# Moving six state factors to TensorE and four transposes to DMAs in a recurrent attention and MoE kernel

## The chip, the cores and the metric

The kernel runs on one core of a Trainium2 chip. The metric is the device time of one execution in microseconds (us), as the median of several runs. The engines are called as the profile calls them: PE (matrix multiplications), PEld (its weight loads), DVE (element by element), ACT (functions and copies), POOL (element by element, and it issues some DMAs) and SP, which here only issues DMAs.

## The reference

```python
# q, k, v, alpha: 4 batches, 8 heads, 768 steps, 48 wide
for t in range(S):
    state = alpha[:, :, t, :, None] * state + np.einsum('bhd,bhe->bhde', k[:, :, t], v[:, :, t])
    y[:, :, t] = np.einsum('bhd,bhde->bhe', q[:, :, t], state)
x = np.ascontiguousarray(attn_out.transpose(0, 2, 1, 3)).reshape(B * S, H * D)   # 3072 x 384
h = x @ w_in                  # 384 x 2048
r = np.maximum(h, 0.0)
out = ((r * r) @ w_out)       # 2048 x 384, float32
```

## The kernel before

**Chunks.** The recurrence is done in 24 chunks of 128 steps, six for each batch. In a chunk the decays are summed as logarithms: ACT takes the logarithm of alpha (line 438), PE multiplies it with a triangle of ones (448), and ACT takes the exponentials of the sums and of their negatives (467 and 471). DVE multiplies them into q and k (495 or 498, 501). q and k are then turned, so that the head dimension lies on the partitions: as eight PE transposes (276) and a DVE copy out of PSUM (395), or by one transposing DMA that SP issues (515). PE makes the scores, DVE masks them (570), PE multiplies them with v and adds q times the state before (both at 273, through a helper). The state is updated by a matmul, multiplied by the decay over the whole chunk (DVE, 604) and copied as bf16 (ACT, 609). ACT copies the chunk's result out of PSUM as x (393 or 414's operand `xn`), and x is turned too: by three PE transposes and a copy, or by a transposing DMA (414).

The decay over a whole chunk, the state factor `ae`, comes in one of two ways. For chunks below `TURN` four matmuls with a single column of ones (450) sum the logarithms, and two small exponentials on ACT (474, 477) write the factors. From `TURN` on the exponential is written as float32 in another order (`Af`, 467), and two small DMAs issued by POOL (484) take its last row. Chunks from `XFROM` on turn q and k by DMA, chunks from `XTURN` on turn x by DMA.

**The first four chunks** are done as two super-chunks of 256 steps (`add_super`), in which every partition holds two steps; their loads are `add_load2` (388), and the copies of the turned q and k are `e_cp` (line 717, costs in line 724), on the engine that the schedule finds free first.

**MoE.** The tokens' first layer is done for groups of chunks (`GN`: four, one, one, then two at a time). A relu on ACT (878) and a square on DVE (886) follow each PSUM bank; then the second layer with the weights in `w_out_b`. ACT copies the result into one of four `held` tiles of four chunks each (953), which share a ring of four buffers with the loads of the weights, and POOL issues the output DMAs (961, 964), the last few SP.

**Order.** A list scheduler in the kernel (`Plan`) sets the order of the instructions on each engine before anything is emitted. Each operation has an engine, or several with a cost for each, an estimated duration, what it depends on and a priority. `gate` keeps the chunks from running further ahead of the MoE than a lead that grows from 3.5 to 6.5 chunks. `OUT_AT + 2.0 * s` is the time in the schedule before which the output of chunk `s` isn't placed; on the chip it only sets its place in POOL's order. `DMA_ORDER` is the order of the first loads on SP. Each engine, and SP as the queue of DMAs, then works through its list in order and waits on semaphores where data isn't there. Before the second layer begins, matmuls on a constant (`warm`) fill holes that the schedule sees on PE.

Of the kernel before, what the change touches and what calls it, by code (L numbers as in the profile page):

```python
# [59 lines left out]
def after(op, x=0.0):  # L60
    return (op, x)
# [103 lines left out]
def kernel(  # L165
# [86 lines left out]
    w_out_b = consts.tile([P, FT, d_model], BF16)  # L252

    NBUF = 4
    TURN = 12
    AE_LAT = 3.6
    L_s = big.tile([P, NBUF, H, DP], BF16)
    nc.gpsimd.memset(L_s[:, :, :, D:], 0.0)
# [10 lines left out]
    def pin(ins):  # L269
        tc.keep_in_program_order(ins)  # L270

    def mm(*a, **kw):
        pin(nc.tensor.matmul(*a, **kw))  # L273
# [23 lines left out]
    def add(eng, dur, emit, *deps, **kw):  # L297
        return plan.add(Op(eng, dur, emit, deps, **kw))
# [47 lines left out]
    SRC = dict(srcs)  # L346
    EARLY = 2 * 3
    PAIRS = 8
    XFROM, XTURN = 12, 14
    LEAD = 3.5  # L350

    NS = 2
# [38 lines left out]
    def cast(op, out_t, in_t):  # L391
        if op.eng == "ACT":
            pin(nc.scalar.copy(out_t, in_t))  # L393
        elif op.eng == "DVE":
            pin(nc.vector.tensor_copy(out_t, in_t))  # L395
        else:
            pin(nc.gpsimd.tensor_copy(out_t, in_t))
# [29 lines left out]
    def add_chunk(s):  # L427
# [18 lines left out]
        def e_p0():  # L446
            pm = d["pm"] = psum(p0, [P, 512], FP32)
            mm(pm[:, 0:HD], lhsT=utri_b[:, 0, :], rhs=L[:, :, 0:D], start=True, stop=True)
            for p in range(NP if s < TURN else 0):
                mm(pm[:, HD + p:HD + p + 1], lhsT=L[:, 2 * p:2 * p + 2, :], rhs=ones_col,  # L450
                   start=True, stop=True)
        p0 = Op("PE", 0.27 if s < TURN else 0.17, e_p0, [ln], takes=GLA_BANKS, lat=0.17, **g)
        p0.gla = s
        d["p0"] = p0

        def split(x, s):
            if s < TURN:
                return x.rearrange("p (h d) -> p h d", h=H)
            return x.rearrange("p (n j d) -> p n j d", n=NP, j=2)

        def e_A():
            if s < TURN:
                d["A"] = work.tile([P, H, D], BF16, name="A")
            else:
                d["Af"] = work.tile([P, 2, D, NP], FP32, name="Af", bufs=2)
                d["A"] = d["Af"].rearrange("p j d n -> p n j d")
            pin(nc.scalar.activation(d["A"], split(d["pm"][:, 0:HD], s), AF.Exp))  # L467
# [10 lines left out]
        plan.add(p0)  # L478
        a_ = add("ACT", 0.38 if s < TURN else 0.76, e_A, p0, **g)
        ai = add("ACT", 0.38, e_Ai, p0, after(a_), **g)  # L480

        def e_aed():
            for j in range(2):
                pin(nc.gpsimd.dma_start(out=ae_s[HF * j:HF * j + D, i, j], in_=d["Af"][P - 1:P, j]))  # L484
        if s < TURN:
            ae0 = add("ACT", 0.18, e_ae0, p0, after(ai), **g)
# [147 lines left out]
    def add_super(u):  # L634

        d = SUP[u]
        i = 2 * u % NBUF
# [3 lines left out]
        g = dict(prio=-10.0 + u * 0.02)  # L641
# [67 lines left out]
        def e_p1(v, w, src):  # L709
            if w == 0:  # L710
                d["pT"][v] = psum(p1[v], [P, 2, NH, 2, 2, HF], BF16)
            for t in any_:
                for n in range(NH):
                    p = NH * v + n
                    tr(d["pT"][v][:, w, n, :, t, :], src[:, t, 2 * p:2 * p + 2, :], ident_bf)

        def e_cp(v):
            d["qk"][v] = work.tile([P, 2, NH, 2, 2, HF], BF16, name="qkT")
            cast(cp[v], d["qk"][v], d["pT"][v])
        p1, cp = [None, None], [None, None]  # L720
        for v in any_:
            p1[v] = plan.add(Op("PE", 0.225, lambda v=v: e_p1(v, 0, qA), [mq[v]], takes=SUP_BANKS, lat=0.15, **g))
            p1k = plan.add(Op("PE", 0.225, lambda v=v: e_p1(v, 1, kI), [mk[v], after(p1[v])], lat=0.15, **g))
            cp[v] = add({"DVE": 0.61, "ACT": 0.92}, 0, lambda v=v: e_cp(v), p1k, **g)
            p1[v].gives = cp[v]
        cq = cp[1]

# [114 lines left out]
    NGT = 3  # L842
    FIRST = sl_bank[4:1:-1]
    M2_LAST = sl_bank[::-1]
    OUT_AT = 118.0
    LAST_COLS = ((0, 256), (256, 384))
    RELU_PRIO = -20.0
    RELU_PRIO0 = 0.0
# [74 lines left out]
    def add_moe2(g, tt, before, box, quarters, pools):  # L923
# [41 lines left out]
        if s < NT - 3:  # L965
            add("POOL", 0.56, e_out, ev, at=OUT_AT + 2.0 * s, lat=2.5, prio=5.0).dma = 0.77
        else:
            add("OUT", 0.55, e_out, ev)
        return op

    DMA_ORDER = ["0 at0 qt0 kt0 at1 qt1 kt1 vt", "1 at0 at1 qt0 kt0 qt1 kt1", "i", "1 vt"] + ["i"] * 5 + ["o"] * 4
    for x in DMA_ORDER + [s for s in range(2 * NS, NT) if s not in DMA_ORDER]:
        if x in ("i", "o"):
            load_w(x)
        elif isinstance(x, str):
            for nm in x[1:].split():
                add_load2(int(x[0]), nm)
            if len(SUP[int(x[0])]) == 2 * len(srcs) - 1:
                add_super(int(x[0]))
        else:  # L980
            for nm, _ in srcs:
                add_load(x, nm)
            add_chunk(x)
# [84 lines left out]
```

## Time and profile before

| | us |
|---|---|
| median of 3 runs (lowest to highest) | 179.23 (179.03 to 179.42) |
| the profiled execution | 179.80 |
| its span, first to last instruction | 178.1 |
| PE busy / weight loads busy | 172.0 / 126.3 |
| DVE / ACT / POOL busy | 124.8 / 122.8 / 53.1 |

The granted clock was 0.999 over the span. Of PE's time, the first layer's matmuls took 72.0 us and the second's 69.8 as the rows count them. The rows of matmuls overlap, since each lasts until its result is out; where the text speaks of what a matmul costs, it takes the distance from its start to the next start. The DMA loads of q, k, v and alpha are 192 KB for each chunk and tensor.

### The profile page before, as it was taken

How to read it: one execution, taken by the hardware profiler on the slowest of the kernel's cores; microseconds unless marked ns; L12 is line 12 of the kernel's file. 1: busy time of each engine (PE TensorE's matmuls, PEld its weight loads, DVE VectorE, ACT ScalarE, POOL GpSimd, SP SyncE). 2: the span in 40 equal slices, each digit the busy share in tenths (PEclk: the TensorE clock that was granted, in tenths of full speed). 3: DMA queues.
4: the chain of work that ended last, by engine and by line, in shares of the span. 5: the costliest groups of instructions: out<-in, count | busy, mean ns of one | idle time of the engine just before them, and what ended most of it. 6: DMA issues, size and time to landing. Idle time of an engine off the chain costs nothing.

```text
span 178.1 us, 4801 instructions
## 1 busy us (share of the span) xinstructions
PE 172.0 (97%) x1866; PEld 126.3 (71%) x1867; DVE 124.8 (70%) x256; ACT 122.8 (69%) x263; POOL 53.1 (30%) x95
## 2 busy tenths in 40 slices
PE   7999999999999999999999999899999999999993
PEld 3567684566896788878766786686688867757862
DVE  6699769936799798998986976798248933800600
ACT  4557789456898689979956698874598947522821
POOL 6023467711110211115222233327736080212000
PEclk9999999999999999999999999999999999999999
DMA  5999999999998999988999799999999969232012
GB/s 128 275 271 322 311 352 377 247 194 213 216 185 156 213 184 203 229 176 155 125 214 209 144 209 109 187 193 239 212 204 294 211 162 212 69 91 89 0 44 88
DMA packets 115798, 34.34 MB, mean 193 GB/s; under 512 B 109840, under 2 KB 114064, under 8 KB 115776
## 3 DMA queue, kind: packets, MB, share of 16 engines
q1 hardware_dynamic: 113536, 29.89, 81.5%
q0 software_dynamic: 2240, 4.15, 7.3%
q8 instruction: 14, 0.23, 0.6%
q14 instruction: 8, 0.07, 0.1%
HBM read 25.17 MB, written 4.72 MB: 168 GB/s over the span
## 4 chain that ended last, share of the span: by engine, by line
PE 79%; DMA 7%; DVE 4%; SPq 3%; ACT 3%; issue 1%; ACTq 0%; DVEq 0%
PE bank L273 71%; PE bank L276 4%; SPq L388 3%; DMA qt<-in_q_dram 3%; DMA at<-in_alpha_dram 3%; PE sc L273 2%; PE st L273 2%; DMA kt<-in_k_dram 2%; ACT r L878 1%; DVE sm L570 1%; ACT Af L467 1%; DVE qkT L395 1%; ACT xn L393 0%; DVE sm L763 0%; DVE xT_big L395 0%
## 5 line engine op out<-in xcount | busy, mean ns | idle before, releaser
L273 PE MATMUL bank<-xT_big,w_in_b 128*128 128x256 bf16 (+2 forms) x599 | 72.0, 268 | 0.3 <-ACT r L878 0.2
L273 PE MATMUL bank<-w_out_b,gT 128*128 128x384 bf16 (+2 forms) x400 | 69.8, 319 | 0.0
L878 ACT ACTIVATE r<-bank 128x512 bf16<-128x512 f32 x96 | 57.0, 611 | 13.5 <-PE bank L273 11.5
L886 DVE TENSOR_TENSOR gT<-r 128x512 bf16<-128x512 bf16 x96 | 46.1, 514 | 23.7 <-ACT r L878 23.4
L273 PEld LDWEIGHTS <-w_in_b 128*128 128x128 bf16 x600 | 53.2, 98 | 11.2 <-issue 1.1
L273 PEld LDWEIGHTS <-gT 128*128 128x128 bf16 x400 | 37.1, 98 | 19.4
L443 POOL CAST vb<-vt 128x384 bf16<-128x384 f32 x20 | 11.1, 553 | 58.1 <-DMA vt<-in_v_dram 30.8
L953 ACT COPY held<-bank 128x384 f32<-128x384 f32 x22 | 10.6, 481 | 14.9 <-PE bank L273 14.6
L484 POOL DMA_DIRECT2D ae_s<-Af x24 | 12.2, 511 | 25.4 <-ACT Af L467 22.2
L570 DVE TENSOR_TENSOR sm<-sc,utri_b 128x512 bf16<-128x512 f32 x24 | 15.4, 684 | 2.0 <-PE sc L273 1.8
L273 PEld LDWEIGHTS <-qkT 64*128 64x128 bf16 (+2 forms) x304 | 10.5, 97 | 5.1 <-issue 2.4
L393 ACT CAST xn<-bank 128x384 bf16<-128x384 f32 x24 | 11.1, 485 | 4.4 <-PE bank L273 4.1
L498 DVE TENSOR_TENSOR qk_s<-qt,Af 128x384 bf16<-128x384 f32 x12 | 10.2, 854 | 4.6 <-ACT Af L467 4.6
L438 ACT ACTIVATE L_s<-at 128x384 bf16<-128x384 f32 x20 | 10.6, 543 | 2.7 <-DMA at<-in_alpha_dram 2.7
L961 POOL DMA_DIRECT2D out_dram<-held x17 | 9.2, 545 | 7.9 <-ACT held L953 7.9
L467 ACT ACTIVATE Af<-bank 128x384 f32<-128x384 f32 x12 | 10.6, 883 | 0.9 <-PE bank L273 0.7
L501 DVE TENSOR_TENSOR qk_s<-kt,Ainv 128x384 bf16<-128x384 f32 x20 | 11.0, 548 | 0.0
L395 DVE COPY qkT<-bank 128x1024 bf16<-128x1024 bf16 (+1 forms) x14 | 8.3, 609 | 3.4 <-PE bank L276 3.4
L609 ACT CAST sb<-st 128x384 bf16<-128x384 f32 x16 | 8.0, 499 | 3.9 <-DVE st L604 3.8
L471 ACT ACTIVATE Ainv<-bank 128x384 bf16<-128x384 f32 x20 | 10.3, 514 | 0.0
L570 DVE TENSOR_TENSOR sm<-bank,utri_b 128x512 bf16<-128x512 f32 x16 | 10.2, 681 | 0.0
L604 DVE TENSOR_TENSOR st<-st,ae_s 128x384 f32<-128x384 f32 x16 | 8.9, 557 | 1.7 <-PE st L273 1.7
(71 smaller groups left out, 165.6 us busy)
## 6 DMA issues: line engine op xcount, KB each, us to landing
at<-in_alpha_dram SPq DMA_DIRECT2D x24, 192.0 KB, 4.0
qt<-in_q_dram SPq DMA_DIRECT2D x24, 192.0 KB, 3.8
kt<-in_k_dram SPq DMA_DIRECT2D x24, 192.0 KB, 4.0
vt<-in_v_dram SPq DMA_DIRECT2D x20, 192.0 KB, 3.9
out_dram<-held POOLq DMA_DIRECT2D x17, 192.0 KB, 4.5
wo<-in_moe_w_out_dram SPq DMA_DIRECT2D x4, 768.0 KB, 7.3
wi<-in_moe_w_in_dram SPq DMA_DIRECT2D x4, 384.0 KB, 6.8
wi<-in_moe_w_in_dram SPq DMA_DIRECT2D x2, 768.0 KB, 5.6
```

What stands on the lines that cost most here:

```text
L273: pin(nc.tensor.matmul(*a, **kw))
L393: pin(nc.scalar.copy(out_t, in_t))
L438: pin(nc.scalar.activation(L[:, :, 0:D], d["at"], AF.Ln))
L443: pin(nc.gpsimd.tensor_copy(d["vb"], d["vt"]))
L467: pin(nc.scalar.activation(d["A"], split(d["pm"][:, 0:HD], s), AF.Exp))
L471: pin(nc.scalar.activation(d["Ai"], d["pm"][:, 0:HD].rearrange("p (h d) -> p h d", h=H), AF.Exp, scale=-1.0))
L484: pin(nc.gpsimd.dma_start(out=ae_s[HF * j:HF * j + D, i, j], in_=d["Af"][P - 1:P, j]))
L501: pin(nc.vector.tensor_mul(kI[:, :, 0:D], d["kt"], d["Ai"]))
L570: pin(nc.vector.tensor_mul(d["sm"][:, hh], d["sc"][hh], utri_b.to_broadcast([P, NP, P])))
L878: pin(nc.scalar.activation(box["r"][:, 0:w], box["ph"][:, 0:w], AF.Relu))
L886: pin(nc.vector.tensor_mul(gT[g][:, f0:f0 + per, lo * P:lo * P + n], r, r))
L953: pin(nc.scalar.copy(box["ob"], box["po"]))
```

## The change

The two ways of making the state factor, and of turning q, k and x, keep their code; the chunks from which they apply are set anew. Chunks 12 to 17 take their state factors from one-column matmuls and two exponentials, with the exponential of the sums in bf16. Chunks 10 and 11 turn q and k by DMA, chunks 12 and 13 turn x by DMA. The copies of the second half of the turned q and k of both super-chunks go to ACT alone. The outputs stand 16 us later in the schedule. The load of super-chunk 1's v stands ahead of the first part of `w_in`, not behind it. The scheduler works all orders out anew.

```diff
-    TURN = 12
+    TURN = 18
...
-    XFROM, XTURN = 12, 14
+    XFROM, XTURN = 10, 12
...
-            cp[v] = add({"DVE": 0.61, "ACT": 0.92}, 0, lambda v=v: e_cp(v), p1k, **g)
+            cp[v] = add({"ACT": 0.92} if (u, v) in [(0, 1), (1, 1)] else {"DVE": 0.61, "ACT": 0.92}, 0, lambda v=v: e_cp(v), p1k, **g)
...
-    OUT_AT = 118.0
+    OUT_AT = 134
...
-    DMA_ORDER = ["0 at0 qt0 kt0 at1 qt1 kt1 vt", "1 at0 at1 qt0 kt0 qt1 kt1", "i", "1 vt"] + ["i"] * 5 + ["o"] * 4
+    DMA_ORDER = ["0 at0 qt0 kt0 at1 qt1 kt1 vt", "1 at0 at1 qt0 kt0 qt1 kt1 vt", "i"] + ["i"] * 5 + ["o"] * 4
```

## The prediction

> **What bounds the kernel now.** I read the busy digits first, then the DMA lines of the page, the chain of waits, and last the timeline where PE's starts stand apart.
>
> ```profile
> PE   7999999999999999999999999899999999999993
> ...
> DMA  5999999999998999988999799999999969232012
> ...
> q1 hardware_dynamic: 113536, 29.89, 81.5%
> ...
> PE 79%; DMA 7%; DVE 4%; SPq 3%; ACT 3%; issue 1%; ACTq 0%; DVEq 0%
> ```
>
> PE is full from the second slice to the end, and the DMA engines are full nearly as long, to about 150 us. So there are two limits. PE's own work sets the end as long as something is ready for it; the DMA engines set when the chunks get ready. A busy digit can hide a wait, so I took the distances between the starts of PE's matmuls against the usual distance of each shape. From 27 us on the matmuls stand at that distance (109 ns for 256 columns, 162 ns for 384), except at 45.3 (0.29 us lost), 69.9 (0.25), 112.7 to 113.2 (0.78) and some of 0.1 to 0.2. About 1.8 us in all: not much is left to win there, and every new wait is paid in full. In the timeline the largest one reads so:
>
> ```profile
> 101.43 1.65 SPq L515 DMA_TRANSPOSE qkT<-qk_s  x1
> ...
> 104.42 2.96 SPq L414 DMA_TRANSPOSE xT_big<-xn  x2
> ...
> 107.44 0.57 SPq L368 DMA_DIRECT2D at<-in_alpha_dram  x1
> ...
> 112.13 0.52 ACT L438 ACTIVATE L_s<-at 128x384 bf16<-128x384 f32 x1 [1.07 <-DMA at<-in_alpha_dram]
> 112.56 1.06 ACT L878 ACTIVATE r<-bank 128x512 bf16<-128x512 f32 x2
> ```
>
> Chunk 20's alpha is issued on SP behind three transposing DMAs, lands 4.7 us later, and ACT stands 1.07 us at its logarithm with the relus queued behind. PE waits first for the logarithm (0.46), then for a relu (0.32).
>
> The start has the other stretch where PE is not fed:
>
> ```profile
> 17.37 0.96 POOL L656 CAST vb<-vt 128x384 bf16<-128x384 f32 x2 [1.16 <-DMA vt<-in_v_dram]
> ...
> 18.36 0.51 PE L273 MATMUL st<-vb,qk_s 64*128 64x96 bf16 x8
> ...
> 19.11 0.81 PE L273 MATMUL bank<-warm 128*128 128x512 bf16 x3 [0.24 <-ACT r L878]
> ```
>
> The second v lands at 17.4 us, its cast frees the state matmuls at 18.36, and PE does matmuls on a constant meanwhile.
>
> **Part by part. PE work.** One chunk in the timeline gives the prices by start to start:
>
> ```profile
> 58.07 0.39 PE L276 MATMUL bank<-ident_bf,qk_s 128*128 128x128 bf16 x4
> ...
> 58.29 0.33 PE L273 MATMUL bank<-L_s,utri_b 128*128 128x384 bf16 x1
> ...
> 58.45 0.24 PE L273 MATMUL bank<-ones_col,L_s 128*128 128x1 bf16 x4
> ...
> 58.56 0.38 PE L276 MATMUL bank<-ident_bf,qk_s 128*128 128x128 bf16 x4
> ```
>
> Four transposes hold PE for 0.22 us (58.07 to 58.29), four one-column matmuls for 0.11 (58.45 to 58.56; 0.10 in other chunks). Removed: two groups of four in chunks 10 and 11 (4 x 0.22 = 0.88) and three x transposes at 0.165 in chunks 12 and 13 (0.33). Added: 6 x 0.105 = 0.63. Net -0.58 us, on the engine that sets the end.
>
> [...] The trace has load rows of 96 to 100 ns but starts 25 ns apart, since the loads run under the matmuls before.
>
> **ACT and DVE.** In six chunks the 883 ns exponential (L467) becomes the 495 ns one and two of 0.17 us are added: -0.05 us each on ACT. The q product falls from 854 to 565 ns: -1.7 us on DVE, which also loses two copies of 685 ns and two of 351 ns. DVE is 70% and ACT 69% busy and neither ends the chain, so I count nothing; the cover is PE's MoE work, without it q and k of each chunk would come 0.7 us earlier. Twelve small DMAs leave POOL (6.1 us of its time), which is 30% busy; nothing.
>
> **The two copies forced to ACT** (L724). The first ran on DVE at 9.98 us, the second at 16.36. ACT has no row of this size; by its rows of 265, 372, 481 ns for 128, 256, 384 elements 1024 take about 1.0 us, against 0.69. Scores come 0.15 to 0.35 us later, the mask products on DVE 0 to 0.6 us earlier, and the logarithms of super-chunk 1 (10.35, 11.10) may queue up to 0.5 behind. Bounds -0.6 to +0.5; taken as 0, the copies being nearest to an even trade.
>
> **Second v before w_in.** v moves past one 384 KB load. That load landed at 15.3 and v 2.05 us later, so v comes 1.2 to 2 us earlier and the first w_in some 2 us later. Its cast then ends near 18.2 instead of 16.2, and the first MoE matmuls go from 17.6 to about 18.3, up to 0.65 us. The fifth w_in load waits for that cast's buffer, but three loads ahead of it land until 20.7, which hides it; without them its landing (22.7) would slip 2 us. Chunk 3's x, which PE awaits at 24.27 (0.29 us), can come up to 1.9 us earlier. What is late next is chunk 4: its logarithm waits for DMA until 34.48 whatever the start does, and its x arrives at 45.12, just as the first group's MoE work runs out (45.2). Chunk 4's first matmul comes 1.6 us after its logarithm ends (36.62 against 35.0), so at most 1.6 us can be kept. Bounds -1.6 to +0.65; I take -0.4, nearer to the 0.29 that PE visibly waits than to the end.
>
> **Four more transposing DMAs.** SP spends at least 1.25 us issuing one of q and k and 1.19 one of x, 4.9 in all. From the DMA packets (256 B, mean 28 ns, 1024 per q and k, 384 per x, 16 engines) they take 1.8 and 0.68 us of all engines: 5.0 us where the DMA share by stage is 0.98 to 1.11 (60 to 100 us). They land 4.4 and 4.0 us after issue (medians), against 1.3 for q and k on PE and DVE (eight transposes 0.61, copy 0.69) and 0.7 for x. Queued behind them on SP are the loads of chunks 14 to 20. Chunks 16, 17 and 18 have slack between logarithm and first matmul (8.9, 10.5 and 5 us); 15, 19 and 20 have 1.2, 1.2 and 0.6. Bounds: -0.8, if the new order removes the stall at 112.7, to +5.0, if nothing hides them. I take 0, nearest to that stall staying as it is, and keep the ends.
>
> **Outputs 16 us later in POOL's order.** Between 120 and 140 us their packets take 6.8 us of the DMA engines; most of that moves later, and the last loads gain it. Their buffers are a ring of four: eviction 16 (144.9) waits for outputs 0 to 3. By the order of POOL now, outputs 0 and 1 would issue before the v cast at 136.2 and 2 and 3 right behind, landed by 142: 3 us of cover; without it ACT and the relus wait. Some twelve outputs run together after 152.6, beside the last x transposes (155.5, 156.8), but 48 matmuls (155.2 to 163.0) hide those.
>
> **Sum.** -0.58 - 0.4 = -0.98 us. On the profiled execution, 179.80 (span 178.1 and 1.7 around it), that is 178.82; the median of the runs, 179.23, is 0.57 lower, so 178.25, and I say 178.2.
>
> **Rivals.**
> - *Slower: x comes too late for the next MoE group.* The group of chunks 12 and 13 begins at 98.2, 0.5 us after its x. By DMA that x comes some 3 us later, while only 8 second-layer matmuls (1.3 us) are then left to do: PE stands 3 - 0.5 - 1.3 = 1.2 us. With SP's 4.9 us more, of which its gaps at 80.5 and 84.2 take up 2.7, chunk 20's alpha is 2.2 us late, 1.0 beyond that: 179.23 - 0.98 + 1.2 to 2.2 = 179.5 to 180.5, say 180.1. It decides once x is over 1.8 us late. For it: the group starts follow the x arrivals by 0.1 to 4 us all along. Against it: the scheduler moves chunk work into such holes, and three loads have 5 to 10 us of slack. Chance 0.26.
> - *The start's gain is lost at 45 us,* since chunk 4 comes when it comes: 179.23 - 0.58 = 178.65. Chance 0.16.
> - *The start gives all 1.6 and the stall at 112.7 goes:* 179.23 - 0.58 - 1.6 - 0.78 = 176.3; with half of both, 177.5. Chance 0.10.
> - *The lighter PE is not lighter:* each group of four new matmuls shows 0.31 us of weight loads; if that binds, +1.86 instead of +0.63: 179.5. Chance 0.08. [...]
>
> **Numbers.** My forecast has 0.40. A measurement of this kernel can tell 0.2% (0.36 us) from no change. Faster takes the forecast and two rivals with little off (0.62), same the last rival and edges (0.09), slower the first and a remainder (0.29). The range runs from 176.8, which cuts the best case, to 180.8, a little past the end of the slower one, as the DMAs' bound lies far beyond it; the likeliest alone spans 177.7 to 178.8.
>
> **What would show it.** Right: q-and-k and x transposes on PE fewer by 16 and 6, one-column matmuls 56 instead of 32; state matmuls of super-chunk 1 before 18 us; chunk 3's x before 23.5; no distance over 0.5 us after 45. Wrong: L_s rows with DMA waits over 1 us on ACT between 80 and 115, PE idle at the start of the group of chunks 12 and 13, or constant matmuls as many as before 24 us.

## The result, and the profile after

The changed kernel takes 187.69 us (median of six runs, 186.63 to 190.03) where the kernel before takes 179.13 (178.61 to 179.99): a ratio of 1.045, interval 1.042 to 1.048. It is slower by 8.6 us, and the prediction had it faster by one. A profile shows one execution, and three of those read below were the longest or nearly the longest of their kernel's runs (after 189.75 us, e1 186.51, e6 188.15), so their lists of waits are those of a long execution.

The page of the profiled execution after (span 188.0 us) has in its busy digits, the digits of its granted clock and its chain:

```profile
PE   7798997999999999999999899999798099999993
...
PEclk9999999999999999999999999999999759999999
DMA  5999799999999979999989998899979797031022
...
PE 61%; DMA 19%; SPq 6%; ACT 3%; DVE 3%; POOL 3%; issue 2%; DVEq 0%; ACTq 0%; POOLq 0%
```

PE has a slice at 0 (the 32nd, 146 to 150 us), the clock digits fall to 7 and 5 right behind it, and DMAs hold 19% of the chain, 7% before. The chain of waits, in order of time, through that slice:

```profile
141.17 4.47 DMA vt<-in_v_dram
...
145.79 0.51 POOL vb L443
146.30 0.98 POOL out_dram L964 x2
147.29 2.13 DMA out_dram<-held
149.42 0.55 DVE held L951
...
150.01 8.90 PE bank L273 x56
```

Read upwards: PE waits for a PSUM bank that DVE empties at 149.42 by eviction 16 (the copy of chunk 16's result into `held`; the scheduler may give these copies to ACT, line 953, or to DVE, line 951). That eviction overwrites a buffer whose outputs, those of chunks 0 to 3, must have landed, and chunk 3's is the last. POOL issues it only at 146.30, because two things stand ahead of it in POOL's order: a pair of state-factor DMAs, for which POOL stands until 143.00, and the cast of the last chunk's v, which SP issued at 141.17. The timeline shows both, and what the wait costs on DVE and PE (the bracket is the idle time ahead and what ended it):

```profile
141.49 0.33 PE L273 MATMUL bank<-L_s,utri_b 128*128 128x384 bf16 x1
...
143.00 1.03 POOL L484 DMA_DIRECT2D ae_s<-Af  x2 [3.13 <-ACT Af L467]
...
144.02 1.05 POOL L964 DMA_DIRECT2D out_dram<-held  x2
...
149.40 0.56 DVE L951 COPY held<-bank 128x384 f32<-128x384 f32 x1 [5.45 <-DMA out_dram<-held]
150.01 4.98 PE L273 MATMUL bank<-xT_big,w_in_b 128*128 128x256 bf16 x24 [4.92 <-DVE held L951]
```

The matmul at 141.49 makes the sums that the state factors wait for. The squares of the MoE stand behind the eviction on DVE, and PE stands 4.92 us. Before, 24 of these matmuls took 2.78 us (in the timeline of `b_again`):

```profile
81.00 2.78 PE L273 MATMUL bank<-xT_big,w_in_b 128*128 128x256 bf16 x24
```

Here they take 4.98, as most start 213 ns apart instead of 109. In the windows by stage, the granted clock (the number behind the five engines) is 0.77 where that happens:

```profile
140.00:150.00 10.00, 5.08 (x62) 4.06 (x61) 2.38 (x5) 4.58 (x9) 6.27 (x13) 0.89 0.95 198
150.00:160.00 10.00, 9.99 (x78) 7.42 (x78) 5.05 (x13) 4.78 (x8) 4.24 (x8) 0.77 0.90 237
```

To see where the whole difference lies, both kernels ran once more on one chip (`b_again`, `a_again` below; spans 177.2 and 186.6). The table sums, over the matmuls of each stretch, by how much each distance to the next start exceeds the median of its shape. The levels depend on how finely the shapes are told apart; the differences between the columns hardly do.

| stretch, us | before | after | what is new after |
|---|---|---|---|
| 0 to 25 | 5.00 | 4.12 | the start gains 0.9 |
| 25 to 35 | 0.23 | 1.88 | casts of w_in (0.70) and w_out (0.96) late |
| 35 to 120 | 5.78 | 6.08 | |
| 120 to 140 | 1.07 | 2.92 | alpha (0.54 and 0.32), masks (0.54 and 0.40) |
| 140 to 160 | 0.59 | 8.24 | the eviction (4.80), then the clock (2.9) |

The differences sum to 10.6 us; the 0.58 by which PE's work is lighter leaves 10.0, and the last matmul starts 9.6 later. Nearly three quarters lie in one wait and its aftermath, the rest in waits for weights, alpha and masks.

### The profile page after: what moved, and what is told of

Same layout as the page of the kernel before. It is cut to its first block, busy times and chain, and to the rows that moved or that the text cites. A ratio compares the mean times of both kernels' runs of the same rounds, so it can differ in the third digit from the quotient of the medians.

```text
span 188.0 us, 4806 instructions
## 1 busy us (share of the span) xinstructions
PE 173.1 (92%) x1866; PEld 125.9 (67%) x1866; DVE 120.2 (64%) x254; ACT 122.1 (65%) x272; POOL 47.6 (25%) x84
## 4 chain that ended last, share of the span: by engine, by line
PE 61%; DMA 19%; SPq 6%; ACT 3%; DVE 3%; POOL 3%; issue 2%; DVEq 0%; ACTq 0%; POOLq 0%
PE bank L273 56%; DMA wi<-in_moe_w_in_dram 8%; SPq L388 5%; DMA wo<-in_moe_w_out_dram 4%; DMA qt<-in_q_dram 2%; DMA vt<-in_v_dram 2%; ACT r L878 2%; PE bank L276 2%; PE sc L273 2%; DMA at<-in_alpha_dram 2%; PE st L273 1%; POOL w_in_b L322 1%; DMA out_dram<-held 1%; DVE sm L570 1%; ACT xn L393 1%
## 5 line engine op out<-in xcount | busy, mean ns | idle before, releaser
L273 PE MATMUL bank<-xT_big,w_in_b 128*128 128x256 bf16 (+2 forms) x600 | 73.6, 273 | 6.3 <-DVE held L951 4.9
L878 ACT ACTIVATE r<-bank 128x512 bf16<-128x512 f32 x96 | 56.2, 608 | 17.9 <-PE bank L273 16.1
L273 PEld LDWEIGHTS <-w_in_b 128*128 128x128 bf16 x600 | 54.1, 99 | 19.1 <-issue 6.8
L886 DVE TENSOR_TENSOR gT<-r 128x512 bf16<-128x512 bf16 x96 | 42.4, 463 | 22.3 <-ACT r L878 21.5
L953 ACT COPY held<-bank 128x384 f32<-128x384 f32 x18 | 8.7, 483 | 16.0 <-PE bank L273 15.8
L961 POOL DMA_DIRECT2D out_dram<-held x17 | 9.1, 542 | 22.2 <-ACT held L953 22.2
L273 PEld LDWEIGHTS <-qkT 64*128 64x128 bf16 (+2 forms) x304 | 10.6, 97 | 4.9 <-issue 2.4
L495 DVE TENSOR_TENSOR qk_s<-qt,A 128x384 bf16<-128x384 f32 x14 | 8.5, 604 | 4.9 <-ACT A L467 4.9
L484 POOL DMA_DIRECT2D ae_s<-Af x12 | 6.2, 523 | 20.8 <-ACT Af L467 15.1
L273 PE MATMUL bank<-vb,sm 128*128 128x48 bf16 (+1 forms) x224 | 9.2, 182 | 0.8 <-DVE sm L570 0.8
L273 PEld LDWEIGHTS <-sm 128*128 128x128 bf16 (+1 forms) x224 | 7.7, 95 | 1.6 <-issue 1.0
```

The lines of the kernel that those rows point to most:

```text
L878: pin(nc.scalar.activation(box["r"][:, 0:w], box["ph"][:, 0:w], AF.Relu))
L886: pin(nc.vector.tensor_mul(gT[g][:, f0:f0 + per, lo * P:lo * P + n], r, r))
L961: pin(q.dma_start(out=out_r[s], in_=box["ob"]))
```

## The experiments

All ratios are to the kernel before on the same chip, with the 95% interval.

### The two kernels again, on one chip

> The kernel before, unchanged, for a profile on the same chip as the runs beside it: ratio 1.00. Theory C (the order was fitted to the chip that it was timed on, and another chip's DMAs use up the cover): waits of PE for transposing DMAs that the first profile of before does not show, together 1 to 3 us.

> The changed kernel, unchanged, on the same chip as the runs beside it: ratio 1.045 as before, with the wait at the eviction of chunk 16 and half-clock matmuls behind it.

Measured: before 0.998 (0.994 to 1.001), 179.29 us; after 1.041 (1.033 to 1.049), 187.54 us. The eviction's wait and the slow matmuls are there again. The 0.78 us at 112.7 that the prediction started from is not in this trace of before; it was one execution's. Nor has this trace a wait of PE for a transposing DMA, so the chip alone does not bring such waits.

### The outputs: is it their place on POOL?

After with the outputs where before had them:

```diff
-    OUT_AT = 134
+    OUT_AT = 118.0
```

> The changed kernel with OUT_AT back at 118, all else changed. Theory A (the eviction of chunk 16 waits for the outputs of chunks 0 to 3, which POOL issues behind the last v casts): the 5.1 us wait at 150 and the 2.2 us of matmuls at half the clock behind it go, 180.0 to 180.8. Theory B (the four more transposing DMAs keep SP and the DMA engines late, and PE would pay the lateness elsewhere if not there): 184 or more.

Measured 1.021 (1.006 to 1.035): the wait and the slow clock are gone, but the time is not that of before. What is left are waits of 0.7 to 1.4 us at 33.8 (for a cast of w_out), 93.6, 109.1, 121.8, 128.4 and 135.7, four of them, from 93.6 to 128.4, ahead of a matmul on a logarithm: ACT's logarithms wait for alpha 13.3 us in 8 times (2.5 us, once, in `b_again`).

After, its order kept but for the eight output DMAs of chunks 0 to 3, which go in front of chunk 22's state factors on POOL:

```diff
...
+    first = [C[s]["out"] for s in range(4)]
+    plan.order = [o for o in plan.order if o not in first]
+    at = plan.order.index(C[22]["ae1"])
+    plan.order[at:at] = first
```

> The changed kernel; on POOL alone the eight output DMAs of chunks 0 to 3 stand ahead of the last-but-one pair of state factor DMAs, three places earlier, so that they are issued near 131 to 135 instead of 138 to 147; nothing else is moved. Theory A: 180.0 to 180.8, as with OUT_AT at 118. Rival (not the place of these eight but the load that all outputs put on the DMA engines after 138 matters): 13 of the outputs still come together after 146, so at most 1.5 us of gain, 186 or more. Theory B: 184 or more.

Measured 1.027 (1.010 to 1.043), and no wait for an output. So it is the place of these eight DMAs that made the eviction wait. By the middle values that is worth about 2 points of the 4.1 to 4.5; the intervals are wide, e2's reaches 1.043, and the after was not measured on this chip, so the size is less sure than the cause. It gave back less than the 7 us at the spot: a logarithm's wait for alpha at 128.5 was 2.34 us in this run, with a half-rate stretch behind it (the mean granted clock of its span is 0.988).

Before with the outputs' time alone changed to 134:

> The kernel before with OUT_AT at 134 alone. Theory A with the prediction's arithmetic (outputs 0 to 3 land by 142, eviction 16 at 144.9): 178.8 to 179.6, the cover is lost only with the rest of the change. Theory A2 (OUT_AT alone is enough, the v casts hold the outputs back here too): a wait at eviction 16 of 1 to 5 us, 180 to 186.

Measured 1.023 (1.012 to 1.034). The timeline of this kernel:

```profile
142.15 0.68 POOL L443 CAST vb<-vt 128x384 bf16<-128x384 f32 x1 [5.07 <-DMA vt<-in_v_dram]
142.77 1.03 POOL L964 DMA_DIRECT2D out_dram<-held  x2
143.79 1.01 POOL L484 DMA_DIRECT2D ae_s<-Af  x2
144.79 1.07 POOL L964 DMA_DIRECT2D out_dram<-held  x2
...
150.67 0.90 PE L273 MATMUL bank<-xT_big,w_in_b 128*128 128x256 bf16 x6 [2.57 <-ACT held L953]
```

The same mechanism with nothing else of the change: outputs behind a cast that waits for its load and behind state-factor DMAs, and PE 2.57 us idle behind the eviction (here on ACT). A second wait of this run, 1.5 us at 101.5, lies far from it.

### The clock: what does the slow stretch cost?

After, with 22 matmuls of 512 columns on a constant ahead of the matmul that waits, so that PE is busy meanwhile. It ran first beside no run of the after, then beside `a_again`:

> The changed kernel with 22 matmuls of 512 columns on a constant (4.75 us at 216 ns) into the free score banks, just ahead of the matmul that waits for the bank of chunk 16's eviction. The wait is not shortened, PE is only kept busy during it. If the slow matmuls after the wait (213 against 109 ns, 21 of them) come from the clock that PE lost while it stood: 187.7 - 2.2 = 185.5, and no matmul over 120 ns behind the wait. If they are slow for another reason: 187.7, within 0.5.

> The changed kernel with the 22 matmuls on a constant in the wait, now beside the changed kernel on one chip. If the clock that PE loses in the wait is worth the 21 slow matmuls: 2.2 us under the changed kernel (1.033 of before). If PE's clock is not the cause: the same as the changed kernel.

Measured 1.050 (1.037 to 1.062) the first time, which without the after beside it says nothing, and 1.038 (1.031 to 1.045) against 1.041 for the after. The second run's timeline:

```profile
143.53 4.91 PE L274 MATMUL sc<-warm 128*128 128x512 bf16 x22
149.15 2.78 PE L274 MATMUL bank<-xT_big,w_in_b 128*128 128x256 bf16 x24 [0.71 <-DVE held L952]
...
156.79 0.40 PE L274 MATMUL bank<-qkT 64*128 64x128 bf16 x8 [0.61 <-DMA qkT<-qk_s]
```

The 24 matmuls are back at 2.78 us: the slow stretch came from PE standing still. But the span fell by only 0.9 of the 2.9 us that the stretch cost in `a_again`: here the outputs landed later, so that PE resumed 1.2 us later (149.15 against 147.92), and PE, early afterwards, waits 0.8 us for a turning DMA at 156.8. The intervals of the two ratios overlap, so the end effect is small or none.

### Each part alone, the order worked out anew

Before, with one part of the change each: v ahead of w_in; `TURN` 18; `XFROM` and `XTURN` 10 and 12; the two copies on ACT.

```diff
e4:  DMA_ORDER: "1 vt" ahead of the first "i"
e5:  TURN = 18
e6:  XFROM, XTURN = 10, 12
e7:  cp[v] = add({"ACT": 0.92} if (u, v) in [(0, 1), (1, 1)] else ...
```

> The kernel before with super-chunk 1's v ahead of the first w_in load, alone. Prediction's step: 0.4 us faster than before (bounds -1.6 to +0.65). Theory A after the result (the first w_in cast comes later, the weights' ring of four buffers lets the fifth and sixth w_in load go later, and the first group's second layer waits for w_in and w_out): 0.3 to 1.0 us slower, with waits of PE for w_in or w_out casts of 0.5 us or more between 26 and 36 us.

> The kernel before with TURN at 18 alone: chunks 12 to 17 by one-column matmuls. Prediction's price: PE +0.63 us, so 0.63 us slower unless the earlier q products save waits; at most 0.8 us faster if the alpha wait at 112 goes. Theory B (the transposing DMAs of chunks 10 to 13 are what holds the chunks up): within 0.8 us of before either way.

> The kernel before with q and k from chunk 10 and x from chunk 12 turned by DMA, alone. Prediction's price: PE -1.21 us if nothing waits. Theory B (four more transposing DMAs put SP's loads of chunks 16 to 22 behind, ACT stands at their logarithms and the relus behind it): 2 to 4 us slower than before (1.1 to 2.2%), with waits of ACT for alpha of 1 us and more between 100 and 140 us. Rival (the lost 3.7 us come from the other parts): faster by 0.5 to 1.2 us.

> The kernel before with the two copies of the turned q and k forced to ACT, alone. Prediction's step: 0, bounds -0.6 to +0.5 us. Rival: the start gains what the changed kernel showed there (its 50th to 90th MoE matmuls came about 1 us earlier), 0.5 to 1 us faster.

| part alone | ratio | largest waits of PE, us |
|---|---|---|
| e4, v ahead of w_in | 1.010 (1.005 to 1.015) | 1.17 at 20.8, and half the clock from 20.7 to 27.5 (2.5 us) |
| e5, TURN | 1.023 (1.014 to 1.031) | 1.70 at 104.6 (logarithm), 1.19 at 154.6 (turning DMA) |
| e6, XFROM and XTURN | 1.014 (1.003 to 1.025) | 2.71 at 161.2 and 1.97 at 144.9 (turning DMAs), 1.5 at 117.9 (relu, behind a logarithm) |
| e7, copies on ACT | 1.011 (1.005 to 1.018) | 2.20 at 125.9 (turning DMA) |

Every part costs 1 to 2.3%, also where it takes work from PE, and the waits stand far from it: two copies at 10 and 16 us should not make a turning DMA late at 126. With `OUT_AT` they add up to 8.1%, nearly twice the whole. That pointed to the newly worked-out order.

### The same parts with the order of before held

The plan of before is kept, and the changed operations are exchanged in it: one-column matmuls and exponentials where the other way of making the factor stood; a transposing DMA where the PE transposes stood.

```diff
h2:
+    for s in range(12, 18):
...
+        ai.emit = lambda f=(e1, e2, e3): [g() for g in f]
+        ae1.emit = lambda: None
h3:
+    for s in (10, 11):
...
+        p1q.emit = cp.emit = lambda: None
+        p1k.emit = turn
+    for s in (12, 13):
...
+        p4.emit, xT.emit = turn, lambda: None
h4:
...
+        SUP[u]["cp_ops"][1].eng = "ACT"
...
+    plan.order.insert(a, plan.order.pop(b))
```

> Chunks 12 to 17 alone take their factors from one-column matmuls, in the order of before. Theory D: PE's price alone, +0.63 us, 1.001 to 1.005. Theory B: as with the order worked out anew, 1.014 to 1.031.

> Chunks 10 and 11 turn q and k, chunks 12 and 13 turn x by DMA, alone, in the order of before. Theory D: between -1.2 us (PE) and a small loss, 0.993 to 1.003. Theory B: the SP queue's 4.9 us more are paid by PE, 1.01 to 1.025, with waits of PE at the scores of chunks 10 to 13, at the first layer of chunks 12 and 13, and behind alpha after 100 us.

> The two copies to ACT and the second v ahead of the first w_in, in the order of before. Theory D: 0.997 to 1.002. Rival (the weights' ring delays w_in and w_out whatever the order): PE waits of 0.5 us or more for w_in or w_out between 20 and 36 us, 1.003 to 1.01.

> All parts of the change but the outputs' place, made in the order of before: the schedule is worked out with the old constants, then the chunks' instructions are exchanged in their places (chunks 12 to 17: factors from one-column matmuls behind the second exponential; chunks 10 and 11: the transposing DMA in place of k's transposes; chunks 12 and 13: in place of x's; two copies to ACT; second v ahead of the first w_in). Theory D (a newly worked out order costs 1 to 2%, the parts do not): 0.994 to 1.004 of before. Theory B (the parts' own costs, above all the four transposing DMAs): 1.015 to 1.025, like the changed kernel with its outputs at 118 (1.0206).

Measured: h2 1.0028 (1.0012 to 1.0045); h3 1.057 (1.054 to 1.061); h4 1.006 (1.004 to 1.008); h1, all three together, 1.052 (1.046 to 1.058; its six runs lie between 187.3 and 191.8 us). h3 and h1 lost more than either theory had.

h2: the factor by one-column matmuls costs 0.45 us (0.2 to 0.8 by the interval), where PE's 24 new matmuls were priced at 0.63. The other 2% of e5 are not the part's own.

h3: in the order of before the four DMAs cost 10 us. That order was made for PE's transposes, so this is their price in it, not one that they have anywhere. The timeline of h3 at chunk 11, ahead of it the same place in before (`b_again`), where PE turns q and k:

```profile
72.84 0.39 PE L276 MATMUL bank<-ident_bf,qk_s 128*128 128x128 bf16 x4
...
74.47 0.40 PE L273 MATMUL sc<-qkT 64*128 64x128 bf16 x8
74.70 0.39 PE L273 MATMUL bank<-qkT 64*128 64x128 bf16 x8
```

```profile
72.92 3.21 SPq L521 DMA_TRANSPOSE qkT<-qk_s  x1
73.45 0.40 PE L273 MATMUL sc<-qkT 64*128 64x128 bf16 x8
...
78.23 0.61 PE L273 MATMUL bank<-qkT 64*128 64x128 bf16 x8 [4.38 <-DMA qkT<-qk_s]
```

Before, the scores of chunk 11 (74.70) follow its last transposes by 1.9 us. In h3 the DMA is issued at 72.92, takes SP 3.21 us and lands at 78.2: PE stands 4.38 us, and the next matmuls run at half rate (18 of 256 columns take 4.02 us, from 78.77; 2.14 in `b_again`, from 75.02). The same happens at 106.55 (2.63 us, for x). With the order worked out anew (e6) PE has other work at these two places and does not wait there; 1.4% is left, in the waits of the table.

h4: the first MoE matmul comes 0.77 us later than in `b_again` (18.00 against 17.24), as the first w_in's cast ends at 17.95, and 0.63 of it stays until 87, where PE waits 0.63 more. The waits for later weights that its rival foretold between 20 and 36 us are not in this trace.

### Does a new order cost something by itself?

Before, with only the scheduler's model changed. The work is the same and only its order differs, but for a few copies and evictions that the scheduler puts on the other of ACT and DVE, and one or two more matmuls on the constant in p1.

```diff
p1:   ACT's latency in the model, 0.14 to 0.15
p2:   WLD = 2.05 to 2.10
e13:  XB of q and k: turn 1.2 to 1.8, lat 2.8 to 3.4;  XB of x: turn 0.5 to 0.7
```

> The kernel before with one number of the schedule's model changed: ACT's latency 0.15 for 0.14. Same instructions, same engines but for a few copies, another order from the first microseconds on. Theory D (the order of before is one that happens to fit, and any new order costs about 1%, whatever the edit): 1.0 to 2.3% slower than before, with waits of PE in new places. Theory B (the edits' own costs make the loss): within 0.4% of before.

> The kernel before with one number of the scheduler's model changed (the time it gives a weight's DMA, 2.05 to 2.10): the same instructions, another order worked out. If a newly worked-out order costs something by itself, as the first such change did (1.0135), this gives 1.005 to 1.02, with waits of 0.8 to 1.5 us in the trace that the order of before has not. If that first case was a single bad draw, it gives 0.998 to 1.003.

> The kernel before with the scheduler told what the traces show of a transposing DMA: 1.8 us of the DMA engines for q or k (1.2 in its model), 0.7 for x (0.5), and 3.4 us to landing in place of 2.8. Same instructions, new order. If new orders cost because the model has these DMAs too short, this order has fewer waits at them and gives 0.99 to 1.003. If any order worked out anew costs, whatever the model says, it gives 1.005 to 1.02.

Measured: p1 1.0135 (1.005 to 1.022); p2 1.001 (0.998 to 1.004); e13 1.056 (1.052 to 1.059).

So a new order is no fixed price; in these three tries it cost from nothing to 5.6%. p1 loses PE 1.13 us at 46.4, its largest wait: in the timeline of p1 the next chunk's sums wait for a PSUM bank that a copy on DVE frees, and that copy waits for one on ACT:

```profile
45.96 0.42 DVE L395 COPY qkT<-bank 128x512 bf16<-128x512 bf16 x1 [0.51 <-ACT qkT L393]
...
46.44 0.32 PE L273 MATMUL bank<-L_s,utri_b 128*128 128x384 bf16 x1 [0.96 <-DVE qkT L395]
```

e13 was meant as the cure, the model told what transposing DMAs cost in the traces. It is the worst of the three, and again by a transposing DMA behind another on SP (timeline of e13):

```profile
149.19 1.07 ACT L393 CAST xn<-bank 128x384 bf16<-128x384 f32 x2 [3.42 <-PE bank L273]
...
149.70 2.14 SPq L515 DMA_TRANSPOSE qkT<-qk_s  x1
...
151.93 2.71 SPq L414 DMA_TRANSPOSE xT_big<-xn  x2
...
157.21 1.03 PE L273 MATMUL bank<-xT_big,w_in_b 128*128 128x256 bf16 x4 [3.88 <-DMA xT_big<-xn]
```

x is ready at 150.3, SP turns q and k first, and x lands at 157.2 with nothing left for PE. My theory that the orders lose because the model has these DMAs too short thus found no support: the truer price did not give a better order. Why one order loses 0.1% and another 5% stays open beyond the waits that each trace names. No variant beat the kernel before.

## Why the prediction was wrong

**The wait of eviction 16** is the step whose failure cost most: PE stood 4.9 us, and the matmuls behind ran slow. I named the wait, with outputs 0 to 3 "landed by 142: 3 us of cover", and costed it at nothing. I had inserted the outputs into POOL's order of before, "right behind" a v cast at 136.2. In the new order outputs 0 and 1 do issue at 137.8, but two state-factor DMAs (143.0) stand ahead of 2 and 3, and the last v's cast (145.8) ahead of 3 as well. The DMAs wait for an exponential whose sums PE makes only at 141.49, the cast for a load that SP issues only at 141.17. Output 3 lands at 149.4 and eviction 16, due at about 144, waits 5.45. The cover was a time read from one order, where the new order was what had to be bounded; I wrote what happens without the cover ("ACT and the relus wait") and gave it no price, and it was neither in the range nor a rival. DVE and the squares waited instead of ACT and the relus.

**The half-rate stretch behind a long wait** had no place in the sum: 2.2 us at the spot in the profile of the after, 2.9 in `a_again`. In these runs waits of PE of 2.3 us and more (2.34, 2.71, 2.73, 2.80, 4.04, 4.59, 4.80; in h1 2.36 and 4.20) each came with half the clock for 3.41 or 6.83 us, part of it within the longer waits, and the matmuls in it lost 1.3 to 2.9 us. Most shorter ones did not (2.20, 1.97, 1.70), but 1.85 in e13 did, and in e4 1.17 with several small waits around it. In `after` the clock was 0.50 from 147.72 to 154.55, and most matmuls of 256 columns started 213 ns apart in it, against 109 at the full clock. How long PE has to stand for that, these runs do not show: 2.34 us were enough in e2 and 1.85 in e13, 2.20 in e7 were not.

**The four transposing DMAs**, taken as 0 with a bound of +5.0: 10 us with the order held (two waits of PE, 7.4 us together by the starts, and the clock), 1.4% where the scheduler fills the holes. The bound came from DMA time alone; a PE that waits in its order for the landing (4.4 us of idle time at 78.2 in h3) can lose more. The rival "x comes too late for the next MoE group" had the mechanism, and h3 shows it at 106.55 as 2.8 us against the 1.2 forecast; in the after it does not come: PE waits for no x there. Its other half, alpha late behind SP's turns, does come: waits at 105.6 and 124.6 of 0.86 and 1.18 on ACT.

**The start.** Its parts came as predicted: the second v's cast at 15.34 instead of 17.37, the first w_in cast at 17.29 instead of 15.30, state matmuls of super-chunk 1 at 16.30, chunk 3's x by 22.2. PE was 1.3 us ahead at 4% of the MoE work and 0.5 behind at 12%. The hiding step failed, "three loads ahead of it land until 20.7, which hides it". The chain of after:

```profile
18.42 0.84 POOL w_in_b L322
...
19.27 7.97 DMA wi<-in_moe_w_in_dram
...
27.30 1.50 POOL w_in_b L322
```

The sixth load waits for a cast's buffer until 19.27 and then takes 8.0 us to land; its cast ends at 28.8 where PE waits 0.70, and w_out's cast, behind it, costs 0.96. I followed the fifth load and not the sixth. The wait for the buffer is not what made it late, though: in `b_again` the sixth load is issued at 19.55, later still, and lands in 5.6 us. Why it took 8.0 here stays open; the DMA engines were busy for only 0.66 of the time between 21 and 23 us. With the same two edits in the order of before (h4) it takes 5.6 us and PE waits for no later weight, so these 1.65 us go with the new order. h4 as a whole costs 1.0 us (0.7 to 1.5), for the start and the two copies, where the forecast was -0.4 and 0 and the bounds together reached +1.15.

**The new order itself** was left out. Where a scheduler works everything out anew, little far from the edit stays in place; each sum of parts that I made was against an order that the changed kernel doesn't have. How much of the after's loss beyond the eviction is due to it was not measured by itself.

**What was right.** The counts, in the groups after:

```profile
L276 PE MATMUL bank<-ident_bf,qk_s 128*128 128x128 bf16 x80 | 7.2, 219 | 1.2 <-DVE qk_s L700 1.0
...
L276 PE MATMUL bank<-ident_bf,xn 128*128 128x128 bf16 x36 | 4.0, 219 | 0.0
L273 PE MATMUL bank<-ones_col,L_s 128*128 128x1 bf16 x56 | 3.4, 164 | 0.0
```

16 and 6 transposes fewer (96 and 42 before), 24 one-column matmuls more (32 before); 0.45 us for these in h2 against 0.63 forecast, so the rival "the lighter PE is not lighter" (+1.86) is out. The weight loads of the one-column matmuls last 95 to 98 ns each in `after`, but run under other matmuls: at 92.08 four of them take 0.31 us together, beside a matmul of 384 columns of 0.32. The copies on ACT took 1.01 us each, as estimated. DVE, ACT and POOL do not bound the kernel by their work: their busy times fell or stayed (120.2, 122.1, 47.6 us) while the span grew by 10.

## What to carry to other kernels

An output DMA that frees a buffer in a ring is on the path of whoever writes that buffer next: before moving it later, list what will stand ahead of it on its issuing queue, and what each of those waits for. Where a scheduler works out the order anew, first measure what an order worked out anew does with the instructions unchanged, and then each part in a held order; the second takes the scheduler's draw out of the comparison, but tells what the part costs in that order only, as h3 against e6 shows. Count the slow matmuls behind a long wait of PE with it: in these traces every wait of 2.3 us or more was followed by matmuls at half the clock, which lost another 1.3 to 2.9 us.

## What was not expected of the hardware

After PE had stood for 2.3 us or longer, the granted clock was 0.50 for 3.41 us or twice that, 6.83, in each of these traces, and in it most matmuls of 256 columns started 213 ns apart (`after`, from 150.01). In `a_again` it was 0.50 from 147.05 to 153.88, where PE resumed at 147.92; after the shorter waits of e2, e3 and h3 (2.34, 2.73, 2.80 us) it fell only 0.2 to 0.8 us after PE had resumed. With the wait filled with constant matmuls (e11b) the granted clock was 1.000 over the span. One SBUF-to-SBUF transposing DMA of q and k took SP from 1.25 us (the shortest of 12 in `before`) to 3.58 (e1, at 127.0) to issue. The program of before had medians of 179.3 to 179.7 us on one chip and 181.5 and 181.9 on two others, which is why each ratio is taken on one chip.
